# Batch 3's u turned on TensorE, v loaded from SyncE's queue, and the last output tile in two halves

## The chip, the cores and the metric

The kernel runs on one core of one Trainium2 chip. The metric is the device time of one execution in microseconds. Three timed runs of the kernel before took 314.05, 314.24 and 315.2 us; the median is 314.24 us. Engines are named as the profile names them: PE (TensorE), DVE (VectorE), ACT (ScalarE), POOL (GpSimd) and SP (SyncE). SP only issues transfers.

## The reference

Eight batches of 576 tokens go through attention with 8 heads of 64 (a band of 32 tokens on each side, and 8 global tokens), and the result x through a mixer: first across the tokens, then across the 512 channels.

```python
mask = np.abs(pos[:, None] - pos[None, :]) <= window          # window = 32
mask = mask | is_global[:, None] | is_global[None, :]
attn = softmax(where(mask, scale * q @ k.T, -1e9))
x = (attn @ v)                                                # [8, 576, 512]
h = np.maximum(xt @ w_tok1, 0.0) @ w_tok2                     # xt: x with tokens last
u = x + h.transpose(0, 2, 1)
out = u + np.maximum(u @ w_ch1, 0.0) @ w_ch2                  # 512 -> 1536 -> 512
```

## The kernel before

Each batch has 576 tokens, handled as four tiles of 128 and a rest of 64; the rests of two batches share a tile of 128 rows. A batch passes these steps.

- `load_qk`, `load_rest`, `load_v` bring q, k and v as float32 (lq, lk, lr, lv: lr holds the rests of q and k, lv has five chunks). ACT casts them to float16 (qk, rn, vsh); DVE copies v to half-shifted rows (`shift_v`, tile vod).
- q and k are turned so that the head dimension lies on the partitions. For batches 0 to 2 PE does it (`turn_pe`); from batch 3 on nine DMA transposes from SP do (`turn_dma`, tiles rawr and raw), and DVE copies each result into qT and kT (L646 to L654).
- `scores` (L673), an exponential on ACT (L683, tile e), a mask on DVE (L689), the sums for the global tokens (L720), `values` (L740, L753), and a division on DVE give x (L781).
- `token1` (L803, tile a) and `token2` (L821) are the mix across tokens; DVE adds x and gives u (L834), and ul for the rest (L837).
- `turn_u` turns u to uT with the channels on the partitions: for b < 3 by four PE transposes a tile (L848) and an eviction by ACT or DVE (L850), otherwise by one DMA transpose a tile from SP (L853). The shared rest is always turned by a DMA transpose (L843, tile uTl).
- `chan1` (L866; L878 for the rest) with a relu (L858, L860; tiles b, b1l), then `chan2` (L895): 12 matmuls a tile of tokens; DVE adds u and writes osb (L903), and POOL, or SP for the last batch and for the rests, stores it (L906, L909).

All this is recorded by `op` as a list of operations, each with the engines it may run on and a cost in microseconds, a priority, and what it reads and writes. `run` then plays a model of the core over the list: at each step it takes the operation with the lowest priority number among those that could start soonest on an engine, and writes out that engine's instruction. So the order on every engine is fixed when the program is built, and a changed cost or engine can move other operations too. At run time each engine works strictly in its written order and waits at semaphores. A transfer issued by SP or ACT also waits for an earlier one of SP or ACT, since completions are counted on eight semaphores that are used in turn.

Eight PSUM banks are shared by everything PE writes; `run` gives a bank to a new result when its former result has been read. There is one lv for all batches, so a chunk of the next batch is loaded once ACT has cast the one before. From batch 3 on q and k are loaded by SP and v by ACT (L942 to L946). With `manual_schedule` nothing else reorders.

The last operations are batch 7's: `chan2` of its four tiles, each stored by SP, and the shared rest of batches 6 and 7, which SP stores in two pieces of 64 rows.

Of the kernel before, what the change touches and what calls it, by code (L numbers as in the profile page):

```python
# [8 lines left out]
F32 = mybir.dt.float32  # L9
# [6 lines left out]
P = 128  # L16
# [11 lines left out]
def kernel(  # L28
# [12 lines left out]
    nc = tc.nc  # L41
    B, H, S, D = q.shape
# [5 lines left out]
    NJ = DCH // P  # L48
    assert S == 576 and D == 64 and DM == 512 and DTOK == 256 and DCH == 1536
    LAST = S - P * (NT - 1)  # L50
# [68 lines left out]
    def run(free, look, hop, warm_until):  # L119
# [41 lines left out]
        def drain(t):  # L161
            if t > clock[0]:
                flow(rings, clock[0], t)
                clock[0] = t
# [28 lines left out]
        while ready:  # L193
            cand = {}
            for i in ready:
                o = ops[i]
                t0, sl = 0.0, None
                if o["new"]:
                    sl = slot(o["new"][0], len(o["new"][1]), max([free["P"]] + list(at[i].values())))
                    if sl is None:  # L200
                        continue
                    t0 = max(t0, max(x[0] for x in sl))
                best = None
                for k, (e, c) in enumerate(o["opts"]):
                    st = max([free[e], t0] + [f + (hop if x != e else 0.0) for x, f in at[i].items()])
                    if o["dma"]:
                        ln, z = lanes["G" if e == "G" else "S"], filled["A" if e == "K" else e]
                        if len(ln) >= 8:
                            st = max(st, max(ln[-8], ln[-7], ln[-6]) + 2.5 if e == "A" else ln[-8])
                        room, x = RING - o["dma"][3], len(z)  # L210
                        while x and room >= z[x - 1][1]:
                            room -= z[x - 1][1]
                            x -= 1
                        if x:
                            st = max(st, z[x - 1][0])
                    if e == "P" and o["mode"] != mode:
                        c = c + 0.095
                    key = (st + c + 0.25 * k, e, st, c)
                    if best is None or key < best:
                        best = key  # L220
                cand.setdefault(best[1], []).append((best[2], o["pri"], i, best[3], sl))
            assert cand, ("stuck", banks, [(ops[i]["opts"], ops[i]["pri"], ops[i]["new"] and ops[i]["new"][1]) for i in ready])
            pick = None
            for e, cs in cand.items():
                lim = min(x[0] for x in cs) + look[e]
                x = min((x for x in cs if x[0] <= lim), key=lambda x: (x[1], x[0], x[2]))
                if pick is None or x[0] < pick[1][0]:
                    pick = (e, x)
            e, (st, _, i, c, sl) = pick
            o = ops[i]  # L230
            if e == "P":
                gap, spare = st - free["P"], [k for k in range(8) if (banks[k][1] is None or not open_uses[banks[k][1]]) and banks[k][0] <= free["P"]]
                if st < warm_until and gap > 0.52 and spare:
                    warm(min(spare, key=lambda k: (banks[k][0], k)), int((gap - 0.3) / (0.22 if st < 12.0 else 0.12)))
                mode = o["mode"]
            if o["new"]:
                kind, keys, shape, dt = o["new"]
                for key, (_, k) in zip(keys, sl):
                    home[key] = [k, k + 1] if kind == "S" else [k]
                    for z in home[key]:  # L240
                        banks[z] = (0.0, key)
                    ps_tile[key] = view(k, shape, dt)
            o["fn"](e)
            free[e] = st + c
            f = st + c + LAT[e]
            if o["dma"]:
                work, size, lag, packets = o["dma"]
                q = "A" if e == "K" else e
                drain(min(f, min(free[x] for x in "GSA")))
                f = land(q, f, work, size, i)  # L250
                filled[q].append((f, packets))
                f += lag
                lanes["G" if e == "G" else "S"].append(f)
                f += o["late"] + (LATE if st > 36.0 else 0.3)
            fin[i] = f
            log.append((st, f, e, i, max(o["deps"], key=lambda x: fin[x]) if o["deps"] else None))
            ready.discard(i)
            for key in o["ps"]:
                open_uses[key] -= 1
                for z in home[key]:  # L260
                    banks[z] = (max(banks[z][0], f + hop), key)
            for u in users[i]:
                left[u] -= 1
                if i in ops[u]["behind"]:
                    at[u][e] = max(at[u].get(e, 0.0), st + c)
                else:
                    x = "D" if o["dma"] else e
                    at[u][x] = max(at[u].get(x, 0.0), f)
                if not left[u]:
                    ready.add(u)  # L270
# [614 lines left out]
    nout = [0]  # L885

    def chan2(b, tau, pri):
        i, key = b % 2, ("o", b, tau)
        last = tau == NT - 1
        js = [range(0, 4), range(4, 8), range(8, 12)] if b == 0 else [range(0, 6), range(6, 12)]  # L890
        for part, jr in enumerate(js):
            def f(e, jr=jr):
                for j in jr:
                    w = b1l[:, j, :] if last else b1[:, j, P * tau : P * tau + P]
                    nc.tensor.matmul(ps_tile[key], lhsT=w, rhs=wc2[:, j, :], start=(j == 0), stop=(j == NJ - 1))  # L895
            r = [("wc2", t) for t in sorted({j // 4 for j in jr})]
            r += [("b1l", t) for t in range(3)] if last else [("b1", j) for j in range(NJ)]
            op([("P", 0.2165 * len(jr))], pri - 0.5 * part if b else pri + 5 * part, f, r=r, ps=[key], new=("M", [key], [P, 512], F32) if part == 0 else None)
        o = nout[0] % 3
        nout[0] += 1  # L900
        osb = osbs[o]
        def g(e):
            nc.vector.tensor_add(out=osb, in0=uls[b // 2 % 2] if last else u16s[i][:, tau], in1=ps_tile[key])  # L903
        op([("V", 0.62)], pri - 8, g, r=[("ul", b // 2 % 2, 0), ("ul", b // 2 % 2, 1)] if last else [("u", i, tau)], ps=[key], w=[("osb", o)])
        if not last:
            op([("G", 0.56) if b < B - 1 else ("S", 0.45)], pri + 5, lambda e: ENG[e].dma_start(out=out[b, P * tau : P * tau + P, :], in_=osb), r=[("osb", o)], dma=STORE)  # L906
        else:
            for z in range(2):
                op([("S", 0.45)], pri + 5, lambda e, z=z: nc.sync.dma_start(  # L909
                    out=out[b - 1 + z, S - LAST : S, :], in_=osb[64 * z : 64 * z + 64]), r=[("osb", o)], dma=(0.39, 2048, 0.8, 64))  # L910
# [11 lines left out]
    def loads(b, n0=0):  # L922
        pl = 100.0 * b - 145 if b != 1 else -174.0
        if b == 0:
            load_rest(0, -196, [("S", 0.65)])
            for hs in (slice(0, 2), slice(2, 4), slice(4, 8)):
                for ti in range(2):
                    load_qk(0, ti, hs, -195 + hs.start, [("S", 0.6)])
            load_v(0, -180, [("S", 0.6)])
            gate(-178, [("lv", NT - 4)], [lv[:, NT - 4, 0, 0:1]])  # L930
            return
        if b < PEB:
            if b == 1:
                pl = -173.9
            load_rest(b, pl, [("G", 0.73)], [n0] if b == 1 else ())
            for h in range(0, H, 4):
                for ti in range(2):
                    load_qk(b, ti, slice(h, h + 4), pl + 1 + h / 2 if b > 1 else pl + 0.1 + h / 100, [("G", 0.88)], [n0] if b == 1 else ())
            if b > 1:
                load_v(b, pl + 6, [("G", 0.87)])  # L940
        else:
            load_rest(b, pl, [("S", 0.65)])  # L942
            for h in range(0, H, 4):
                for ti in range(2):
                    load_qk(b, ti, slice(h, h + 4), pl + 1 + h / 2, [("S", 0.5)])
            load_v(b, pl + 6, [("A", 0.6)])  # L946

    def casts(b):
        pc = 100.0 * b - 140
# [6 lines left out]
    for b in range(B):  # L956
        base = 100.0 * b
        ca = base - 85
# [53 lines left out]
        for tau in range(NT):  # L1012
            token2(b, tau, ca + tau)
            if tau < NT - 1 or b % 2:
                turn_u(b, tau, ca + tau + 2, b < 3)
        if b and b % 2 == 0:
            chan2(b - 1, NT - 1, base + 24)
        for j in range(NJ):
# [40 lines left out]
```

## Time and profile before

| | |
|---|---|
| median of three timed runs | 314.24 us |
| profiled execution | 314.6 us |
| its span, first to last instruction | 312.9 us |
| PE / DVE / ACT / POOL busy in it | 292.0 / 186.8 / 180.5 / 60.5 us |
| mean granted PE clock | 0.987 of full speed |
| transfers: SP and ACT queues (q1, q10), POOL queue (q0) | 26.49 and 5.90 MB, 18.45 MB |

"L895 PE MATMUL bank<-wc,b" is a group of instructions by line of the kernel, engine, operation, what it writes and what it reads. In the views that list a timeline, a row has the start and the duration in us, the engine, the line and, in brackets, how long the engine stood idle before it and what released it; SPq and ACTq are transfers issued by SP and ACT, whose duration is that of the issue. A row of the windows view has the stretch, its length, the busy time and number of instructions of PE, PEld (weight loads), DVE, ACT and POOL, then the granted PE clock, the share of the transfer engines and GB/s. Batch b's channel step runs beside the scores of batch b + 1 and the transposes of batch b + 2: around 100 us PE is at token2 of batch 2, and around 136 us at that of batch 3.

### The profile page before, as it was taken

What the parts mean: (1) busy time and instruction counts of PE and PEld (TensorE: products, weight loads), DVE (VectorE), ACT (ScalarE), POOL (GpSimd) and SP (SyncE); (2) the same over time, 40 slices, a digit from 0 to 9 for tenths busy, and PEclk for the clock granted to TensorE, in tenths of its full rate; (3) what the DMA queues carried; (4) which work ended last, traced back from release to release, by engine and by line L of the source; (5) the groups of instructions that cost most, each with busy time, mean ns of one, the idle gap of its engine ahead of it and who ended that gap; (6) DMA issues with size and microseconds to landing.
All of it is one profiled execution on the core that took longest, in us unless ns stands there. A gap on an engine that the chain in (4) does not pass through costs nothing.

```text
span 312.9 us, 7276 instructions
## 1 busy us (share of the span) xinstructions
PE 292.0 (93%) x2943; PEld 154.4 (49%) x2943; DVE 186.8 (60%) x410; ACT 180.5 (58%) x325; POOL 60.5 (19%) x109
## 2 busy tenths in 40 slices
PE   6979889997999979988999998999999999999994
PEld 4755545454474434533456444544555445444641
DVE  7789667569686674876675846964543357230021
ACT  4864895377987758841989376733742083305500
POOL 8589635632001100002000110002000200020000
PEclk9989999999999979999999999999999999999998
DMA  6989999999999999999979999924003211051013
GB/s 183 255 129 287 208 222 222 287 243 234 214 212 220 194 267 318 118 190 221 325 114 176 203 313 189 159 50 136 36 0 63 89 53 37 12 140 69 2 67 102
DMA packets 94660, 51.31 MB, mean 164 GB/s; under 512 B 73698, under 2 KB 89954, under 8 KB 94626
## 3 DMA queue, kind: packets, MB, share of 16 engines
q1 hardware_dynamic: 62480, 26.49, 40.3%
q0 software_dynamic: 8704, 18.45, 24.0%
q10 hardware_dynamic: 23442, 5.90, 11.1%
q8 instruction: 23, 0.38, 0.5%
q14 instruction: 11, 0.09, 0.1%
HBM read 36.11 MB, written 9.44 MB: 146 GB/s over the span
## 4 chain that ended last, share of the span: by engine, by line
PE 58%; DMA 26%; ACT 5%; DVE 5%; issue 2%; SPq 2%; POOL 1%; POOLq 0%; ACTq 0%; DVEq 0%
PE bank L895 22%; PE bank L866 21%; DMA lv<-in_v_dram 8%; DMA raw<-qk 6%; DMA lq<-in_q_dram 5%; PE bank L821 4%; DMA g_q<-in_q_dram,idx_i 3%; PE bank L673 3%; PE bank L803 2%; DMA lk<-in_k_dram 2%; PE bank L878 2%; ACT qk L534 2%; ACT vsh L546 2%; DVE osb L903 2%; PE bank L753 1%
## 5 line engine op out<-in xcount | busy, mean ns | idle before, releaser
L866 PE MATMUL bank<-uT,wc 128*128 128x512 f16 x384 | 94.0, 384 | 6.4 <-DVE osb L903 2.3
L895 PE MATMUL bank<-wc,b 128*128 128x512 f16 x384 | 88.3, 379 | 2.9 <-DVE osb L903 2.2
L858 ACT ACTIVATE b<-bank 128x512 f16<-128x512 f32 x88 | 52.5, 617 | 38.3 <-PE bank L866 38.3
L683 ACT ACTIVATE e<-bank 128x648 f16<-128x648 f32 x64 | 42.7, 737 | 30.0 <-PE bank L673 29.8
L895 PEld LDWEIGHTS <-b 128*128 128x128 f16 x384 | 36.7, 98 | 45.9 <-issue 4.2
L866 PEld LDWEIGHTS <-wc 128*128 128x128 f16 x384 | 35.2, 98 | 48.5 <-issue 8.7
L906 POOL DMA_DIRECT2D out_dram<-osb x28 | 16.1, 574 | 203.1 <-DVE osb L903 203.0
L903 DVE TENSOR_TENSOR osb<-u,bank 128x512 f32<-128x512 f16 x32 | 21.9, 686 | 45.3 <-PE bank L895 41.5
L546 ACT CAST vsh<-lv 128x512 f16<-128x512 f32 (+3 forms) x44 | 26.5, 620 | 9.7 <-DMA uT<-u 5.3
L689 DVE TENSOR_TENSOR e<-e,masku 128x1296 f16<-128x1296 f16 x28 | 23.3, 831 | 13.7 <-ACT e L683 13.2
L834 DVE TENSOR_TENSOR u<-x,bank 128x512 f16<-128x512 f16 x30 | 18.7, 681 | 15.0 <-PE bank L821 14.8
L781 DVE TENSOR_TENSOR x<-bank,rr 128x512 f16<-128x512 f32 x32 | 22.1, 691 | 1.1
L821 PE MATMUL bank<-a,w 128*128 128x512 f16 x80 | 20.1, 379 | 0.5 <-DVE a L809 0.3
L534 ACT CAST qk<-lq 128x512 f16<-128x512 f32 x26 | 16.2, 626 | 4.5 <-DMA lq<-in_q_dram 2.0
L803 PE MATMUL bank<-x,w 128*128 128x512 f16 x64 | 18.7, 379 | 0.0
L673 PEld LDWEIGHTS <-kT 64*128 64x128 f16 x576 | 11.2, 97 | 14.4 <-issue 13.6
L534 ACT CAST qk<-lk 128x512 f16<-128x512 f32 x27 | 16.9, 631 | 1.8 <-DMA lk<-in_k_dram 1.8
L654 DVE COPY qT<-raw 128x512 f16<-128x512 f16 x20 | 12.0, 602 | 7.2 <-DMA raw<-qk 7.1
L753 PEld LDWEIGHTS <-e 128*64 128x64 f16 x576 | 16.1, 116 | 0.1
L740 PE MATMUL bank<-rf,lf 128*64 128x264 f16 x144 | 15.6, 293 | 0.5 <-DVE rf L726 0.5
L753 PE MATMUL bank<-vsh,e 128*64 128x66 f16 x320 | 16.0, 199 | 0.0
L673 PE MATMUL bank<-qT,kT 64*128 64x72 f16 x576 | 15.4, 198 | 0.0
(164 smaller groups left out, 333.6 us busy)
## 6 DMA issues: line engine op xcount, KB each, us to landing
out_dram<-osb POOLq DMA_DIRECT2D x28, 256.0 KB, 4.3
lq<-in_q_dram SPq DMA_DIRECT2D x11, 512.0 KB, 6.4
lk<-in_k_dram SPq DMA_DIRECT2D x11, 512.0 KB, 7.9
lv<-in_v_dram ACTq DMA_DIRECT2D x15, 256.0 KB, 4.6
wc<-in_moe_w_ch_dram POOLq DMA_DIRECT2D x6, 512.0 KB, 12.8
lq<-in_q_dram POOLq DMA_DIRECT2D x4, 512.0 KB, 6.4
lk<-in_k_dram POOLq DMA_DIRECT2D x4, 512.0 KB, 11.0
lv<-in_v_dram ACTq DMA_DIRECT2D x10, 192.0 KB, 3.8
```

Of the source, the lines that this page charges most:

```text
L534: COPY[e](out=qk[:, ti, p].rearrange("q i (r d) -> q r i d", r=2), in_=(lq, lk)[ti][:, hs])
L546: COPY[e](out=vsh[i][a:z, c, :, 0:D], in_=lv[a:z, c])
L673: nc.tensor.matmul(ps_tile[keys[z]][:, u // 3, UW * (u % 3) : UW * (u % 3) + UW], lhsT=kT[r, 64 * u : 64 * u + P], rhs=qT[r, u // 2, UW * ...
L683: op([("A", 0.595)], pri + 1, lambda e, par=par: nc.scalar.activation(out=es[i][:, 2 * p + par].rearrange("p (n u) x -> p n u x", n=3), in ...
L689: op([("V", 0.85)], pri + 2, lambda e: nc.vector.tensor_mul(out=e2, in0=e2, in1=masku.unsqueeze(1).to_broadcast([P, 2, NB, UW])), r=["mask ...
L753: nc.tensor.matmul(o[:, VW * hh : VW * hh + VW], lhsT=es[i][:, h, 2 * tau + c, x : x + 64], rhs=vod[i][:, tau, h, :] if c else vsh[i][:, t ...
L803: nc.tensor.matmul(ps_tile[key][:, tt], lhsT=w, rhs=x16s[i][:, ch, :], start=(ch == 0), stop=(ch == NT - 1))
L821: nc.tensor.matmul(ps_tile[key], lhsT=w2[:, ch, P * tau - sh : P * tau - sh + P], rhs=a1[:, ch, :], start=(ch == 0), stop=(ch == 1 and not ...
L858: nc.scalar.activation(out=out, in_=in_, func=AF.Relu)
L866: nc.tensor.matmul(ps_tile[key], lhsT=wc1[:, cc, P * j : P * j + P], rhs=uT[:, cc, :], start=(cc == 0), stop=(cc == 3))
L895: nc.tensor.matmul(ps_tile[key], lhsT=w, rhs=wc2[:, j, :], start=(j == 0), stop=(j == NJ - 1))
L903: nc.vector.tensor_add(out=osb, in0=uls[b // 2 % 2] if last else u16s[i][:, tau], in1=ps_tile[key])
```

## The change

Four edits. `turn_u` is called with PE for b < 4 instead of b < 3, so batch 3's four full tiles of u are turned by PE. `load_v` of batches 3 to 7 goes to SP instead of ACT, with a cost of 1.0 in the model instead of 0.6; the cost of a `load_qk` on SP becomes 1.15 instead of 0.5. The last tile, the shared rest of batches 6 and 7, is made in two halves of 256 columns, each with 12 matmuls of 256 columns, its own PSUM bank and its own add; of each half SP stores the 64 rows of batch 6 and ACT those of batch 7. And in the model a transfer issued by ACT holds SP for a time that grows with its packets; after the change this touches only the stores of the last tile.

```diff
@@ run
             if o["dma"]:
                 work, size, lag, packets = o["dma"]
                 q = "A" if e == "K" else e
+                if e == "A":
+                    free["S"] = max(free["S"], st) + 0.9 * o["dma"][3] / 1024
                 drain(min(f, min(free[x] for x in "GSA")))
@@ chan2
         last = tau == NT - 1
+        if last and b == B - 1:
+            osb = osbs[nout[0] % 3]
+            for z in range(2):
+                cs, kz = slice(256 * z, 256 * z + 256), ("o", b, tau, z)
+                def f(e, cs=cs, kz=kz):
+                    for j in range(NJ):
+                        nc.tensor.matmul(ps_tile[kz], lhsT=b1l[:, j, :], rhs=wc2[:, j, cs], start=(j == 0), stop=(j == NJ - 1))
+                op([("P", 1.31)], pri + z, f, r=[("wc2", t) for t in range(3)] + [("b1l", t) for t in range(3)], ps=[kz], new=("M", [kz], [P, 256], F32))
+                op([("V", 0.4)], pri - 8, lambda e, cs=cs, kz=kz: nc.vector.tensor_add(out=osb[:, cs], in0=uls[b // 2 % 2][:, cs], in1=ps_tile[kz]),
+                   r=[("ul", b // 2 % 2, 0), ("ul", b // 2 % 2, 1)] + ([] if z else [("osb", nout[0] % 3)]), ps=[kz], w=[("osbz", z)])
+                for y in range(2):
+                    op([("SA"[y], 0.45)], pri + 5 + z, lambda e, y=y, cs=cs: ENG[e].dma_start(
+                        out=out[b - 1 + y, S - LAST : S, cs], in_=osb[64 * y : 64 * y + 64, cs]), r=[("osbz", z)], dma=(0.25, 1024, 0.8, 64))
+            return
@@ loads
-                    load_qk(b, ti, slice(h, h + 4), pl + 1 + h / 2, [("S", 0.5)])
-            load_v(b, pl + 6, [("A", 0.6)])
+                    load_qk(b, ti, slice(h, h + 4), pl + 1 + h / 2, [("S", 1.15)])
+            load_v(b, pl + 6, [("S", 1.0)])
@@ the loop over batches
-                turn_u(b, tau, ca + tau + 2, b < 3)
+                turn_u(b, tau, ca + tau + 2, b < 4)
```

The order of other instructions moves with it. In the lists below a line number of the new kernel is 2 higher than the old one up to `chan2`, and 16 higher behind it.

SP, around the transposes of batch 4 (rawr from the rests rn, raw from qk; the lq and lk ahead load batch 4). Before:

```order
L643 DMA_TRANSPOSE raw<-qk 128x4x128 x4
L504 DMA lq<-in_q_dram 128x4x256
L504 DMA lk<-in_k_dram 128x4x256
L639 DMA_TRANSPOSE rawr<-rn 128x4x128
L643 DMA_TRANSPOSE raw<-qk 128x4x128 x8
```

After:

```order
L645 DMA_TRANSPOSE raw<-qk 128x4x128 x5
L506 DMA lk<-in_k_dram 128x4x256
L506 DMA lq<-in_q_dram 128x4x256
L506 DMA lk<-in_k_dram 128x4x256
L525 DMA lv<-in_v_dram 96x8x64
L525 DMA lv<-in_v_dram 128x8x64 x3
L525 DMA lv<-in_v_dram 96x8x64
L641 DMA_TRANSPOSE rawr<-rn 128x4x128
L645 DMA_TRANSPOSE raw<-qk 128x4x128 x8
```

Five loads of batch 4's v now stand ahead of its nine transposes, and one load of k has gone behind the last transposes of batch 3.

DVE, at the outputs of batch 1 (osb from u_1, batch 1's u) beside the copies of batch 4's turned q and k into qT_72 and kT_74. Before:

```order
L903 TENSOR_TENSOR osb_104<-u_1_95,bank 128x512
L654 COPY qT_72<-raw 128x4x128
L903 TENSOR_TENSOR osb_102<-u_1_95,bank 128x512
L651 COPY kT_74<-raw 128x512
L654 COPY qT_72<-raw 128x4x128
L651 COPY kT_74<-raw 128x512
L654 COPY qT_72<-raw 128x4x128
L903 TENSOR_TENSOR osb_103<-u_1_95,bank 128x512
L689 TENSOR_TENSOR e_81<-e_81,masku 128x1296
```

After:

```order
L919 TENSOR_TENSOR osb_104<-u_1_95,bank 128x512
L648 COPY qT_72<-rawr 128x4x64
L650 COPY kT_74<-rawr 128x4x64
L556 COPY vod_78<-vsh_76 64x2112
L919 TENSOR_TENSOR osb_102<-u_1_95,bank 128x512
L653 COPY kT_74<-raw 128x512
L919 TENSOR_TENSOR osb_103<-u_1_95,bank 128x512
L656 COPY qT_72<-raw 128x4x128 x2
L691 TENSOR_TENSOR e_81<-e_81,masku 128x1296
```

The last output of batch 1 stood behind five copies from raw and now stands behind one, the second of the eight transposes; a copy of batch 4's v (vod_78) has come ahead of it.

DVE, between x and the first output of the next stage, at batch 3 (u_1 and ul_97 are batch 3's, osb from u_0 is batch 2's, kT_75 and qT_73 batch 5's). Before:

```order
L651 COPY kT_75<-raw 128x512
L654 COPY qT_73<-raw 128x4x128
L860 TENSOR_SCALAR b_100<-bank 128x512
L625 COPY gT<-bank 128x128
L628 COPY kgz<-bank 64x16x8 x2
L633 COPY qT_72<-gT 128x20x8
L651 COPY kT_75<-raw 128x512
L633 COPY qT_73<-gT 128x20x8
L654 COPY qT_73<-raw 128x4x128
L834 TENSOR_TENSOR u_1_95<-x_1_92,bank 128x512 x4
L837 TENSOR_TENSOR ul_97<-x_1_92,bank 64x512
L903 TENSOR_TENSOR osb_102<-u_0_94,bank 128x512
```

After:

```order
L862 TENSOR_SCALAR b_100<-bank 128x512
L627 COPY gT<-bank 128x128
L630 COPY kgz<-bank 64x16x8 x2
L635 COPY qT_72<-gT 128x20x8
L648 COPY qT_73<-rawr 128x4x64
L650 COPY kT_75<-rawr 128x4x64
L656 COPY qT_73<-raw 128x4x128
L653 COPY kT_75<-raw 128x512
L836 TENSOR_TENSOR u_1_95<-x_1_92,bank 128x512 x4
L839 TENSOR_TENSOR ul_97<-x_1_92,bank 64x512
L653 COPY kT_75<-raw 128x512
L656 COPY qT_73<-raw 128x4x128
```

The first row of the old list has four more copies ahead of it (rawr's pair, a vod copy and a raw copy); in the new one the copies of two raw tiles come ahead of u instead of five, and two more between ul and the output.

## The prediction

> **What bounds the kernel now.** I read the page first: its shares and its chain.
>
> ```profile
> span 312.9 us, 7276 instructions
> PE 292.0 (93%) x2943; PEld 154.4 (49%) x2943; DVE 186.8 (60%) x410; ACT 180.5 (58%) x325; POOL 60.5 (19%) x109
> ```
>
> PE is the bound, with 20.9 us idle in the span. The second view, PE's waits from 95 to 200 us, says where idle time is left that this change can reach (before 95 us the queues hardly differ, and after 200 us the list of PE's waits is empty):
>
> ```profile
> PE bank L895 <- DVE osb L903: 2.2, 2, 1.8
> PE bank L866 <- DVE osb L903: 2.1, 1, 2.1
> PE bank L720 <- DVE eg L692: 0.8, 1, 0.8
> PE bank L895 <- ACT b1l L858: 0.4, 1, 0.4
> PE bank L895 <- DVE u L834: 0.2, 1, 0.2
> PE bank L821 <- DVE b L860: 0.2, 1, 0.2
> ```
>
> That is 5.9 us, and it is DVE that is late, not a load as such. The third view, PE's granted clock in short windows, adds a hidden cost:
>
> ```profile
> 113.00:114.00 1.00, 0.73 (x2) 0.24 (x2) 0.96 (x3) 0.00 (x0) 0.49 (x1) 0.66 0.90 199
> 114.00:115.00 1.00, 1.00 (x3) 0.15 (x1) 1.00 (x3) 0.00 (x0) 0.05 (x1) 0.50 0.99 187
> 115.00:116.00 1.00, 1.00 (x20) 0.69 (x20) 0.97 (x4) 0.79 (x2) 0.00 (x0) 0.50 0.73 150
> 116.00:117.00 1.00, 1.00 (x4) 0.39 (x3) 1.00 (x3) 1.00 (x2) 0.00 (x0) 0.63 1.01 369
> ...
> 142.00:144.00 2.00, 2.00 (x10) 0.91 (x10) 1.97 (x4) 0.40 (x1) 0.56 (x1) 1.00 1.31 240
> ```
>
> After the 2.1 us stop the clock (third number from the end) is 0.66, 0.50, 0.50, 0.63, so 0.34 + 0.50 + 0.50 + 0.37 = 1.71 us of work is lost. After the 1.8 us stop at 141.9 it stays 1.00. So the first stop costs 2.08 + 1.71 = 3.79 us, and all of them together 7.6 us. The Trainium skill ("TensorE: Matmul & The Clock Gate", "What's actually happening") has the clock halve after an idle window of about 3.4 us; by that a 2.1 us stop costs no clock, and the sum below would lose 1.71 us of gain. The trace shows 0.50 after 2.1 us, so the trace decides.
>
> Why PE stops there is read from DVE's and SP's timelines:
>
> ```profile
> 107.52 0.61 DVE L651 COPY kT<-raw 128x512 f16<-128x512 f16 x1 [0.26 <-DMA raw<-qk]
> 109.65 0.62 DVE L654 COPY qT<-raw 128x512 f16<-128x512 f16 x1 [1.52 <-DMA raw<-qk]
> 112.03 0.59 DVE L654 COPY qT<-raw 128x512 f16<-128x512 f16 x1 [1.25 <-DMA raw<-qk]
> 112.54 0.68 DVE L903 TENSOR_TENSOR osb<-u,bank 128x512 f32<-128x512 f16 x1
> ```
>
> ```profile
> 97.22 0.57 SPq L504 DMA_DIRECT2D lq<-in_q_dram  x1
> 97.84 0.50 SPq L504 DMA_DIRECT2D lk<-in_k_dram  x1
> 98.45 1.19 SPq L639 DMA_TRANSPOSE rawr<-rn  x1
> 99.75 12.26 SPq L643 DMA_TRANSPOSE raw<-qk  x8
> ```
>
> DVE works strictly in order. The add at 112.54 frees the PSUM bank that PE's chan1 of batch 2 needs; it stands behind copies of batch 4's transposes, which SP issues one per 12.26 / 8 = 1.53 us. The second lands at 107.52, the fifth at 112.03, and only the fifth lets the add go.
>
> **The change part by part.** The sum is made against the profiled execution, 312.9 us of span and 314.6 us in all, 0.4 us over the median of 314.24; differences are carried to the median.
>
> *1. The stop at 111 us.* In the new DVE order this add waits for the second raw tile of batch 4 instead of the fifth; rawr and one vod copy stand ahead of it too. But SP now issues five loads of batch 4's v ahead of rawr; each waits until ACT has cast batch 3's v out of the same buffer, and behind them on SP stand all nine transposes, for which DVE waits. What one costs on SP is not in this stretch of the trace. The nearest rows:
>
> ```profile
> L523 ACTq DMA_DIRECT2D lv<-in_v_dram x25: 337/391/1265, 69.2 to 199.4; - x25
> 5.57 9.06 SPq L523 DMA_DIRECT2D lv<-in_v_dram  x5
> 105.00:113.00 8.00, 6.06 (x65) 2.60 (x64) 4.78 (x10) 5.15 (x10) 1.23 (x2) 1.00 1.27 222
> ```
>
> Below, 0.39 us each, as on ACT; above, 9.06 / 5 = 1.81, as on SP at the start. I take 0.57, the load on SP at 97.22, same queue and moment. The second tile then lands at 107.52 + 5 x 0.57 = 110.4, the bank is free at 110.4 + 0.60 + 0.68 = 111.7 instead of 113.2, 1.5 us earlier, and with the stop at 0.6 us the clock stays up. Gain 1.5 + 1.71 = **3.2 us**. Bounds: 3.8 at 0.39 (the stop gone), and at 1.81 the tile lands at 116.6, 4.6 us after 112.03: a loss of 4.6. What the 25 moved issues free on ACT is not on the path: ACT mostly waits for PE there.
>
> *2. The stop at 142 us.* DVE again:
>
> ```profile
> 134.75 0.61 DVE L654 COPY qT<-raw 128x512 f16<-128x512 f16 x1 [2.50 <-DMA raw<-qk]
> 137.96 2.48 DVE L834 TENSOR_TENSOR u<-x,bank 128x512 f16<-128x512 f16 x4
> 140.47 0.69 DVE L837 TENSOR_TENSOR ul<-x,bank 64x512 f16<-64x512 f16 x1
> 141.19 0.69 DVE L903 TENSOR_TENSOR osb<-u,bank 128x512 f32<-128x512 f16 x1
> ```
>
> Between batch 3's x and that add the new order has one vod copy (0.70) and one raw copy (0.60) less, and only the first two tiles of batch 5 ahead of u. But PE comes earlier by part 1, and SP's stream of batch 5 again has v loads ahead. Bounds: the whole 1.78 + 0.19 + 0.16 = 2.1 us won, or none. I take **1.0 won**, the middle, since DVE's own work shrinks by 1.3.
>
> *3. u of batch 3 on PE.* Added 16 transposes of 128x128; removed four DMA transposes on SP:
>
> ```profile
> 101.63 0.32 PE bank L848 x4
> 292.54 2.69 PE bank L878 x48
> 138.68 5.15 SPq L853 DMA_TRANSPOSE uT<-u  x4
> L850 ACT COPY uT<-bank 128x512 f16<-128x512 f16 x11 | 6.3, 589 | 2.4 <-PE bank L848 2.3
> ```
>
> The same instruction took 0.32 / 4 = 0.08 us, a stream of that size 2.69 / 48 = 0.056. So 0.9 to 1.3 us; I take **1.3 lost**. Four evictions of 0.59 go to ACT, 2.4 us, covered by PE's 36 matmuls of chan2 that stand there anyway (7.8 us); without that cover they would cost the 2.4. The 5.15 us that SP wins only makes batch 6's loads earlier, which nothing waits for at 138 us: nothing.
>
> *4. v on SP in the later batches.* The one stop there, at 192 us, hangs on a transpose:
>
> ```profile
> 181.25 2.10 SPq L639 DMA_TRANSPOSE rawr<-rn  x1
> 190.33 0.23 DVE L646 COPY qT<-rawr 128x256 f16<-128x256 f16 x1 [2.03 <-DMA rawr<-rn]
> ```
>
> Now lk and five v loads stand between uT and this rawr, and PE comes 3.2 + 1.0 - 1.3 = 2.9 us earlier. Between the 0.8 us stop vanishing and 5 x 0.57 = 2.9 us being added, I take **0.7 lost**, because the uT ahead of them, waiting for u, also moves earlier with PE.
>
> *5. The tail.*
>
> ```profile
> 295.23 12.96 PE bank L895 x60
> 308.22 0.69 DVE osb L903
> ...
> 308.93 1.12 SPq L909 DMA_DIRECT2D out_dram<-osb  x2
> DMA to landing us min/median/max: 2.3/2.3/2.4
> ...
> L789 DVE TENSOR_TENSOR x<-bank,rr 64x256 f16<-64x256 f32 x16 | 6.8, 422 | 0.4
> lv<-in_v_dram ACTq DMA_DIRECT2D x15, 256.0 KB, 4.6
> ```
>
> 24 matmuls of half the width keep the array as long as 12 (12 x 0.216 = 2.6). The last add covers 256 columns: 0.42 instead of 0.69. The two last stores start together at 308.65 instead of the second at 308.93 + 0.56 = 309.5. **0.86 won**, if a store from ACT lands as one from SP. If it took the 4.6 us of ACT's loads, it would land at 313.2 instead of 311.8: 1.4 lost.
>
> Sum: -3.2 - 1.0 + 1.3 + 0.7 - 0.9 = -3.1 us, so 314.24 - 3.1 = **311.1 us**.
>
> **The rivals.** *A, slower: v's loads hold up the transposes behind them.* The place is part 1; it decides from (112.03 - 107.52) / 5 = 0.90 us per load. For it: SP's own v loads took 1.81, and five of them are 1152 KB, 5.3 us at the 222 GB/s of that window, 1.06 each, if what follows waits for their data. Against: its q and k loads took 0.5 to 0.6 in that stretch. At 1.06 the tile lands at 112.8, the bank comes 0.8 us later than before, the clock falls as before, and part 2 wins nothing: +0.8 + 1.3 + 0.7 - 0.9 = +1.9, **316.1 us**; at 1.81, 320. The Trainium skill ("DMA: Bandwidth & Descriptors", "Queues, rings and completion order") bears on it: an engine takes turns between queue rows, so v on a row of its own shares, while on SP's row what comes later queues behind it; this trace shows no v on SP beside transposes.
>
> *B, no change: the gain is given back.* PE's order is fixed and the transposes of batches 5 to 7 come at SP's pace; if they don't move, PE waits at 192 us for what it won, and only the tail is left: 314.24 - 0.9 = **313.4 us**. For it: the chain before 192 runs over a raw transpose. Against: SP is rid of 5.15 us at 138 us, and ACT of all issues, so the pace can move.
>
> *C, more: all the stops go.* -7.6 + 1.3 - 0.9 = -7.2, **307.0 us**. For it: DVE's copies are spread; against: every copy ahead of an add is still a possible wait.
>
> **How the numbers follow.** Forecast 0.56, A 0.14, B 0.17, C 0.13. The range leaves out A and the lowest of C, 307.2 to 314.8. About 0.5% (1.6 us) is what a measurement here can tell from no change. Faster: C 0.13, nearly all of the forecast 0.54, a little of B 0.03, together 0.70; same 0.17; slower 0.13.
>
> **What would show it.** Right: no clock window under 0.9 between 105 and 120 us, PE's wait for osb there under 1 us, SP's v loads near 0.6 us each, the last store issued by 308.7 less what was won. Wrong: v loads on SP over 0.9 us, a raw copy with a wait of 2 us ahead of an osb add, or a stop of over 2 us at L720 or L866 later. A stop in front of token2 of batch 2 (near 98 us), where the order now has the last tile of batch 3 ahead of the first add, would be one that I have left at nothing (its 0.4 us stop stays).

## The result, and the profile after

The changed kernel takes 322.69 us (median, 322.39 to 324.27) against 314.24 us: 1.027 times the kernel before, with a 95% interval of 1.0235 to 1.0304. Forecast were 311.1 us. The change costs 8.4 us where 3.1 were to be won. Times in this document are medians of all runs of a kernel, and ratios compare its fast runs alone, since some runs lie over 1.5% above the fastest of their kernel.

The first two rows of the page, to be read beside those of before:

```profile
span 322.5 us, 7368 instructions
PE 294.0 (91%) x2971; PEld 156.0 (48%) x2971; DVE 187.6 (58%) x410; ACT 182.9 (57%) x330; POOL 60.5 (19%) x109
```

PE is busy 2.0 us more and idle 28.5 us in place of 20.9. PE's waits over the whole span (us in total, times, the longest one); the rows left out at the "..." are waits of 1.9 us each on qT and rf:

```profile
PE bank L911 <- DVE u L836: 3.3, 1, 3.3
PE bank L722 <- DVE eg L694: 3.2, 3, 2.0
PE bank L868 <- DVE osb L919: 2.9, 1, 2.9
...
PE bank L911 <- DVE osb L919: 1.5, 1, 1.5
PE bank L823 <- DVE osb L919: 1.4, 1, 1.4
```

It is still DVE that is late. Where the time goes, batch by batch, shows the start of the pair of divisions that completes x of a batch (the `x` rows of DVE at L789 before, L791 after), read from both timelines:

| | x of batch 2 | 3 | 4 | 5 | 6 | 7 | end of the span |
|---|---|---|---|---|---|---|---|
| before, us | 91.6 | 128.5 | 163.5 | 199.0 | 229.3 | 264.9 | 312.9 |
| after, us | 93.5 | 130.4 | 166.2 | 209.6 | 239.7 | 275.3 | 322.5 |
| late by | 1.9 | 1.9 | 2.8 | 10.6 | 10.4 | 10.4 | 9.6 |

Of the 9.6 us, 7.8 arise between x of batch 4 and x of batch 5. The place on which the forecast's largest term rested, between x of batches 2 and 3, neither wins nor loses.

The trace points to SP. All v loads in one row, and SP's timeline where batch 4's v stands ahead of its transposes:

```profile
L525 SPq DMA_DIRECT2D lv<-in_v_dram x30: 449/1237/4781, 5.6 to 193.1; - x30
```

```profile
97.16 0.57 SPq L506 DMA_DIRECT2D lk<-in_k_dram  x1
97.78 0.50 SPq L506 DMA_DIRECT2D lq<-in_q_dram  x1
98.33 0.51 SPq L506 DMA_DIRECT2D lk<-in_k_dram  x1
98.93 7.74 SPq L525 DMA_DIRECT2D lv<-in_v_dram  x5
106.78 1.32 SPq L641 DMA_TRANSPOSE rawr<-rn  x1
108.66 10.96 SPq L645 DMA_TRANSPOSE raw<-qk  x8
```

The q and k loads take 0.5 to 0.57 us, as the forecast took for v as well. The five v loads behind them take 7.74 / 5 = 1.55 us each, and rawr goes out at 106.78 in place of 98.45. DVE then stands still for it, with the adds that PE wants behind:

```profile
113.15 0.23 DVE L648 COPY qT<-rawr 128x256 f16<-128x256 f16 x1 [6.46 <-DMA rawr<-rn]
...
114.28 0.69 DVE L919 TENSOR_TENSOR osb<-u,bank 128x512 f32<-128x512 f16 x1
114.89 0.60 DVE L653 COPY kT<-raw 128x512 f16<-128x512 f16 x1
115.40 0.68 DVE L919 TENSOR_TENSOR osb<-u,bank 128x512 f32<-128x512 f16 x1
```

The first of these adds frees PE, only at 115.0 (the stop of 2.88 us, L868). Batch 3 shows the same earlier: its v loads stand on SP from 69.46 us on, its rawr goes out at 80.99 in place of 77.90, and rf, which PE needs, stands behind the copies:

```profile
86.53 0.23 DVE L648 COPY qT<-rawr 128x256 f16<-128x256 f16 x1 [1.21 <-DMA rawr<-rn]
...
87.96 0.70 DVE L728 TENSOR_TENSOR rf<-bank,blk 128x528 f16<-128x528 f32 x1
```

Before, these two rows stood at 83.88 and 86.43; PE now stops for 1.42 us ahead of L742. Batch 6 shows it on a larger scale. SP, with the row of the kernel before for the same eight transposes behind it:

```profile
150.05 1.34 SPq L506 DMA_DIRECT2D lk<-in_k_dram  x1
151.49 9.03 SPq L525 DMA_DIRECT2D lv<-in_v_dram  x3
...
164.15 2.93 SPq L641 DMA_TRANSPOSE rawr<-rn  x1
167.18 11.57 SPq L645 DMA_TRANSPOSE raw<-qk  x8
```

```profile
159.57 11.37 SPq L643 DMA_TRANSPOSE raw<-qk  x8
```

Three v loads took 9.03 us, and batch 6's transposes start 7.6 us later than before, while x of batch 4 is only 2.8 us later. What DVE and PE make of it:

```profile
178.70 0.59 DVE L656 COPY qT<-raw 128x512 f16<-128x512 f16 x1 [0.60 <-DMA raw<-qk]
179.32 2.48 DVE L836 TENSOR_TENSOR u<-x,bank 128x512 f16<-128x512 f16 x4
181.72 0.67 DVE L839 TENSOR_TENSOR ul<-x,bank 64x512 f16<-64x512 f16 x1
182.32 0.67 DVE L919 TENSOR_TENSOR osb<-u,bank 128x512 f32<-128x512 f16 x1
```

```profile
180.06 1.46 PE L911 MATMUL bank<-wc,b 128*128 128x512 f16 x6 [3.33 <-DVE u L836]
183.04 5.34 PE L911 MATMUL bank<-wc,b 128*128 128x512 f16 x24 [1.52 <-DVE osb L919]
```

u of batch 4 stands behind seven copies from raw, the last of which waits for a transpose until 178.70; PE stops for 3.33 and 1.52 us. In the kernel before, five such copies stood ahead of this u, and u waited for PE, not for a copy; the written order has changed here too. At 187.35 the five loads of batch 7's v follow, and PE stops again, for 2.02 us from 199.1 on, behind a copy from rawr at 199.91 for which DVE had waited 4.00 us.

### The profile page after: what moved, and what is told of

It reads as the page before. It is cut to its first block, busy times and chain, and to the rows that moved or that the text cites. A ratio compares the mean times of both kernels' runs of the same rounds, so it can differ in the third digit from the quotient of the medians.

```text
span 322.5 us, 7368 instructions
## 1 busy us (share of the span) xinstructions
PE 294.0 (91%) x2971; PEld 156.0 (48%) x2971; DVE 187.6 (58%) x410; ACT 182.9 (57%) x330; POOL 60.5 (19%) x109
## 4 chain that ended last, share of the span: by engine, by line
PE 48%; DMA 17%; ACT 15%; DVE 12%; issue 4%; SPq 2%; POOL 0%; ACTq 0%
PE bank L911 17%; PE bank L868 16%; ACT e L685 5%; DMA lk<-in_k_dram 4%; DMA raw<-qk 4%; DMA rawr<-rn 4%; ACT b L860 3%; PE bank L823 3%; DMA g_k<-in_k_dram,idx_i 2%; PE bank L805 2%; PE bank L675 2%; ACT vsh L548 2%; PE bank L755 2%; PE bank L880 2%; PE bank L742 2%
## 5 line engine op out<-in xcount | busy, mean ns | idle before, releaser
L868 PE MATMUL bank<-uT,wc 128*128 128x512 f16 x384 | 93.8, 383 | 5.4 <-DVE osb L919 2.9
L868 PEld LDWEIGHTS <-wc 128*128 128x128 f16 x384 | 35.2, 98 | 47.3 <-issue 8.8
L742 PE MATMUL bank<-rf,lf 128*64 128x264 f16 x144 | 15.4, 290 | 2.4 <-DVE rf L728 1.9
L653 DVE COPY kT<-raw 128x512 f16<-128x512 f16 x20 | 12.0, 599 | 5.4 <-DMA raw<-qk 5.2
```

Source lines behind the costliest of these rows:

```text
L868: nc.tensor.matmul(ps_tile[key], lhsT=wc1[:, cc, P * j : P * j + P], rhs=uT[:, cc, :], start=(cc == 0), stop=(cc == 3))
```

## The experiments

Three theories were set against each other. Theory 1, later called Q: v on SP's queue makes the transposes late. Theory 2: u of batch 3 on PE costs the time. Theory 3: the new written order is bad by itself. Ratios are to the kernel before, timed beside it on the same chip, with 95% intervals.

| kernel | us | ratio | interval |
|---|---|---|---|
| changed | 322.69 | 1.0269 | 1.0235 to 1.0304 |
| v on SP alone | 326.35 | 1.0474 | 1.0392 to 1.0556 |
| the same, v ahead of q and k | 315.76 | 1.0073 | 1.0025 to 1.012 |
| changed, v ahead of q and k | 313.84 | 0.9952 | 0.9918 to 0.9986 |
| changed, model's queue 2600 packets | 319.25 | 1.0168 | 1.0104 to 1.0231 |
| changed, half of v | 309.72 | 0.9813 | 0.9766 to 0.986 |
| before, half of v | 310.38 | 0.9885 | 0.982 to 0.995 |
| changed, raw told 4 us later | 324.44 | 1.0266 | 1.0216 to 1.0315 |
| changed, u of batch 3 by DMA | 324.43 | 1.0348 | 1.028 to 1.0416 |
| v ahead, u of batch 3 by DMA | 314.91 | 1.0013 | 0.9979 to 1.0048 |
| u on PE and halved tail, v on ACT | 317.62 | 1.0164 | 1.0082 to 1.0246 |
| halved tail alone | 313.47 | 0.9977 | 0.9917 to 1.0036 |
| halved tail, raw told 2 us later | 313.39 | 0.9957 | 0.992 to 0.9995 |
| v ahead, raw told 2 us later | 312.81 | 0.9978 | 0.9941 to 1.0014 |
| changed order, v issued by ACT | 339.08 | 1.0869 | 1.0758 to 1.098 |

**v on SP alone** (the kernel before with one edit):

```diff
-                    load_qk(b, ti, slice(h, h + 4), pl + 1 + h / 2, [("S", 0.5)])
-            load_v(b, pl + 6, [("A", 0.6)])
+                    load_qk(b, ti, slice(h, h + 4), pl + 1 + h / 2, [("S", 1.15)])
+            load_v(b, pl + 6, [("S", 1.0)])
```

> The kernel before with the third part of the change alone: v of batches 3 to 7 on SP's queue, with the model costs that go with it (1.0 for v, 1.15 for q and k). Theory 1 (a load of v holds SP for 1.2 us and more, since the queue is full, so the transposes behind it come late and DVE and PE wait): the whole loss and the tail's gain on top, 322 to 325 us, with stops of 2 us and more of PE behind DVE copies of raw. Theory 2 (the loss comes from u of batch 3 on PE, its evictions on ACT and the PE time): 314 us, no stop of 3 us near 178 us.

It takes 326.35 us, more than the whole change and more than either theory expected. So this edit alone makes the loss, and more. The parts don't simply add up: beside it the other edits give some of it back, and without it they cost 1.6% (u on PE and halved tail, below). Its v loads are as dear as in the changed kernel:

```profile
L523 SPq DMA_DIRECT2D lv<-in_v_dram x30: 339/1450/3502, 5.9 to 198.6; - x30
```

**The changed order, v issued by ACT** (only the engine that issues batch 3 to 7's v is put back):

```diff
-                ENG[e].dma_start(
+                (nc.scalar if b >= 3 else ENG[e]).dma_start(
                     out=lv[r0:r1, c], ...
```

> The changed kernel with the same written order on every engine, but each load of v of batches 3 to 7 is issued by ACT at its place in that order instead of by SP. Theory 1 (the price of v on SP's queue): the transposes come as early as before, 312 to 315 us. Theory 3 (the new order, made with other costs, is bad by itself, whichever queue carries v): 319 us or more.

All theories missed: 339.08 us. ACT's timeline and PE's show why it says little about the order:

```profile
116.63 0.34 ACTq L525 DMA_DIRECT2D lv<-in_v_dram  x1
117.01 0.62 ACT L536 CAST qk<-lq 128x512 f16<-128x512 f32 x1 [6.97 <-DMA raw<-qk]
```

```profile
118.65 0.58 PE L850 MATMUL bank<-ident,u 128*128 128x128 f16 x4 [6.60 <-ACT uT L852]
```

ACT stands for 6.97 us ahead of a v load, which the profile puts down to a completion of SP's transposes (the two share the semaphores that count completions), and the evictions of uT, for which PE waits, stand behind it: 6.60 us. In this run the order written for SP holds up ACT's computing. Theory 3 stays untested by it.

**u on PE and the halved tail, without v**, and **the tail alone** (the changed kernel with these lines put back; the second also with the last pair):

```diff
-                if e == "A":
-                    free["S"] = max(free["S"], st) + 0.9 * o["dma"][3] / 1024
-                    load_qk(b, ti, slice(h, h + 4), pl + 1 + h / 2, [("S", 1.15)])
-            load_v(b, pl + 6, [("S", 1.0)])
+                    load_qk(b, ti, slice(h, h + 4), pl + 1 + h / 2, [("S", 0.5)])
+            load_v(b, pl + 6, [("A", 0.6)])
...
-                turn_u(b, tau, ca + tau + 2, b < 4)
+                turn_u(b, tau, ca + tau + 2, b < 3)
```

> The changed kernel without the move of v: u of batch 3 on PE and the halved last tile, v on ACT and the model costs as before. Theory 1: 16 transposes on PE cost up to 1.3 us, the tail wins 0.9, so 313.5 to 315 us; less, if the stop at 142 us goes. Theory 2 (u on PE causes the loss): 320 us or more.

> The kernel before with the last tile in two halves stored by SP and ACT, nothing else. All theories: 0.9 us faster (313.3 us), the last store issued about 0.85 us earlier; if ACT's store landed like its loads of v, 1.4 us slower.

317.62 and 313.47 us; the first lies between what the two theories expected. The tail wins 0.2%, which the interval doesn't tell from nothing. u on PE costs some 4 us here by the medians, and 1.9%, nearer 6 us, by the ratios: three times or more the 1.3 that were taken. A wait that the kernel before doesn't have is u itself: PE's transposes of batch 3's u stand in PE's order and wait for DVE.

```profile
138.53 0.40 PE L848 MATMUL bank<-ident,u 128*128 128x128 f16 x4 [2.53 <-DVE u L834]
```

**Half of v** (in the changed kernel, and in the kernel before; heads 4 to 7 of v of batches 3 to 7 are left out, so these two kernels don't compute the reference; bytes and pieces of v are halved, and the instructions stay):

```diff
+                hs = slice(0, 4 if b >= 3 else H)
-                    out=lv[r0:r1, c], in_=v[b, :, j0 : j0 + (r1 - r0), :].rearrange("h p d -> p h d")
+                    out=lv[r0:r1, c, hs], in_=v[b, hs, j0 : j0 + (r1 - r0), :].rearrange("h p d -> p h d")
```

> The changed kernel, but v of batches 3 to 7 is loaded for heads 0 to 3 only (the other half of lv keeps batch 2's values), so each of the 25 loads on SP has half the pieces and bytes; number and order of all instructions stay. Theory Q (SP's queue takes an issue at once while little is outstanding in it, and makes SP wait when much is; what costs is the amount of v in front of the transposes in one queue): the five issues at 98.9 us took 7.74 us and fall by more than half, to 2.5 to 3.5 us; batch 4's transposes start about 4 us earlier; the time falls from 322.7 to between 313 and 317. Theory S (a v load is dear to issue on SP in itself, per issue): the issues stay at 1.2 us and more, 7 us for the five, and the time stays at 320 to 323. If the price goes by pieces alone, the five take 3.9 us.

> The kernel before (v on ACT), but v of batches 3 to 7 is loaded for heads 0 to 3 only; the other half of lv keeps batch 2's values. It tells whether the 309.7 us of the half-v run on SP came from less traffic in general or from less in SP's queue. Theory Q: on ACT's row the bytes hardly matter to SP's transposes, 312 to 315. Theory B (the transfer engines as a whole are the limit, busy over 90% up to 200 us): this kernel gains as well, 306 to 310.

```profile
94.74 5.44 SPq L526 DMA_DIRECT2D lv<-in_v_dram  x5
```

The five issues at this place fall from 7.74 to 5.44 us only, not to 2.5 to 3.5, but the kernel falls by 13 us, to 309.72, below all theories. PE's waits from 80 to 215 us (this kernel's lines are one higher than the changed kernel's) show that the stops of 3.33, 2.88 and 2.02 us are gone:

```profile
PE bank L824 <- ACT a L815: 2.1, 1, 2.1
PE bank L912 <- DVE osb L920: 0.8, 1, 0.8
PE bank L743 <- ACT b L861: 0.6, 1, 0.6
PE bank L824 <- DVE osb L920: 0.2, 1, 0.2
```

The kernel before gains too, 1.15% or 3.6 us (310.38 us), so less traffic helps on ACT's row as well: theory B holds in part. The pair is what counts: with half of v the change as a whole costs nothing (0.9813 against 0.9885, intervals that overlap), with the whole of v 2.7%. The amount of v on SP is what costs, not the number of issues. It is also the test of theory 3: the written order on every engine is that of the changed kernel, so the order by itself, with less v in SP's queue, loses nothing.

**v ahead of q and k**:

```diff
-            load_v(b, pl + 6, [("S", 1.0)])
+            load_v(b, pl - 0.9, [("S", 1.0)])
```

> The changed kernel with v's priority ahead of the q and k loads of its batch: five v loads stand in front of lk, lq, lk and batch 4's transposes; for later batches the plan puts v directly behind the last batch's transposes. Theory Q: of the five v loads the first two take about 0.5 us, and the three q and k loads behind them, 0.57, 0.50 and 0.51 us in the changed kernel, take over 1 us each; rawr starts at 107 us, give or take 1, as it does now. Later batches' transposes have had more time, so the time falls a little, 316 to 321. Theory S: every v load takes 1.2 us or more, the q and k loads stay at 0.5 to 0.6 us, and rawr starts at 107 us too; 320 to 323.

313.84 us: the whole loss is gone with one priority, better than either theory had it. Which issues are long goes with what is already in the queue:

```profile
97.39 3.98 SPq L525 DMA_DIRECT2D lv<-in_v_dram  x5
101.42 0.85 SPq L506 DMA_DIRECT2D lk<-in_k_dram  x1
102.31 0.54 SPq L506 DMA_DIRECT2D lq<-in_q_dram  x1
102.90 0.61 SPq L506 DMA_DIRECT2D lk<-in_k_dram  x1
103.63 2.46 SPq L641 DMA_TRANSPOSE rawr<-rn  x1
```

The same eight loads take 97.16 to 106.67 us in the changed kernel, 9.5 us, and 97.39 to 103.51, 6.1 us, in this one. The trace's packets show how full the queue was. A q or k load here makes 512 packets of 1 KB, a v load 768 or 1,024 of 256 bytes, a transpose 512 of 256 bytes; with these numbers SP's issues add up to the 80,384 data packets of queue q1. Packets issued less packets finished, at the start and the end of each issue:

```
changed kernel                          v ahead of q and k
start   us    load  at start  at end    start   us    load  at start  at end
 97.2  0.57   lk       502      574      97.4  0.53   lv       489      839
 97.8  0.50   lq       537     1024      98.0  0.49   lv       780     1792
 98.3  0.51   lk      1024     1523      98.6  0.53   lv      1791     2621
 98.9  0.45   lv      1510     2178      99.2  0.95   lv      2541     2596
 99.5  1.38   lv      2148     2712     100.3  1.10   lv      2488     2224
101.0  2.61   lv      2682     2715     101.4  0.85   lk      2172     1946
103.7  1.22   lv      2629     2531     102.3  0.54   lq      1910     1949
105.0  1.67   lv      2425     2292     102.9  0.61   lk      1912     1931
```

Counted so from 40 us on, the fullest that SP's queue became was 2,582 to 2,755 packets in the nine kernels with the whole of v on SP, and 2,085 at most in those with v on ACT. Over the nine kernels, the 40 v loads that began with fewer than 1,000 packets outstanding took 0.47 to 0.64 us each; of the 87 that began with 2,000 or more, 75 took over 1 us. In between both kinds stand, 33 of 98 over 1 us, so the runs show no sharp threshold; at 61.63 us of the changed kernel a q load that began with 2,046 packets took 4.58 us. While such an issue lasts, SP waits with all that follows.

q and k are few packets with many bytes, v many packets with few. That v's loads have to wait for the 1.5 MB of q and k where these stand in front would explain why v in front is quicker; no run shows it by itself. Theory Q was right on the first loads (0.53, 0.49) and wrong on what follows: q and k stay at 0.85 us and less, and rawr goes out at 103.63, not at 107. Theory S falls, for a v load of 1,024 packets takes 0.49 us at 98.0 here and 4.78 at 155.74 in the changed kernel. The gain comes at batch 6, whose rawr copies go from 169.94 to 165.17, so that u of batch 4 starts at 173.42 in place of 179.32, with seven copies from raw ahead of it as in the changed kernel; this u stops PE no longer:

```profile
172.79 0.60 DVE L656 COPY qT<-raw 128x512 f16<-128x512 f16 x1 [0.31 <-DMA raw<-qk]
173.42 2.48 DVE L836 TENSOR_TENSOR u<-x,bank 128x512 f16<-128x512 f16 x4
```

Part of that lead is another order of the loads too: one v load of batch 6 goes out 20 us sooner, and batch 7's rests later. And the written order of DVE and ACT moves with the priority. How much is the queue's fullness and how much the rest isn't separated.

**v on SP alone, ahead of q and k**, the first experiment with only v's priority changed (the edit is shown against that kernel):

```diff
-            load_v(b, pl + 6, [("S", 1.0)])
+            load_v(b, pl - 0.9, [("S", 1.0)])
```

> The kernel before with one edit, v of batches 3 to 7 on SP, placed ahead of q and k of its batch (model costs 1.0 and 1.15 us). The same edit with v behind q and k took 326.3 us (1.047). If the place in SP's queue is what costs, nearly all of that goes: 313 to 317. If the u and tail edits are what made the other v-first kernel good (313.8), this one stays slow: 320 to 327.

315.76 us in place of 326.35, and the median v load 0.90 in place of 1.45 us. By the ratios, v's place, with the order that moves with it, is worth 4.0 of the 4.7% that the edit costs; 0.7% is left.

```profile
L523 SPq DMA_DIRECT2D lv<-in_v_dram x30: 338/897/3378, 6.2 to 184.7; - x30
```

**The model told of the queue** (`RING`, the number of packets that the model lets a queue hold):

```diff
-    RING, LATE = 4096, 2.0
+    RING, LATE = 2600, 2.0
```

> The changed kernel with one number of the planner's model changed: a queue holds 2600 packets at most, in place of 4096 (counted from the trace of the changed kernel, SP's queue never held over 2,715 outstanding packets, and issues become long when it holds over 2,000). SP's written order then puts parts of v between the transposes. Theory Q (the price of v on SP is its place in a queue that is full): the issues of lv fall below 1 us in the median (1.24 in the changed kernel), and the time falls to 312 to 318. Theory S (the loads are dear wherever they stand): 320 to 324.

319.25 us, just above the range of theory Q. SP's order now mixes v loads and transposes, the median v load falls to 0.93 us, and 3.4 us of the 8.4 come back. The number that the model took for the queue is part of why its order was bad, not all.

**The model told that q's and k's transposes land later** (by 4 us in the changed kernel, by 2 us in the kernel with the halved tail and in the one with v ahead; the argument is added to both kinds of transposes):

```diff
-                    r=[("qk", ti, p)], w=[("raw", ti, p)], dma=TURN)
+                    r=[("qk", ti, p)], w=[("raw", ti, p)], dma=TURN, late=4.0)
```

> The changed kernel, but the model is told that the DMA transposes of q and k land 4 us later. SP's order hardly changes; on DVE the adds of osb and u move ahead of copies from raw. Theory D (the late transposes cost PE time because DVE's written order has their copies in front of the adds that PE waits for): PE's stops at 115 us (2.9 us) and 180 us (3.3 us) go below 1 us each and the time falls to 314 to 319. Against it (the turned q and k are themselves needed that soon): those stops are replaced by stops of PE's scores on qT or kT, and the time stays at 321 to 325.

> The kernel before with the last tile in two halves, v on ACT, u as before, and the model told that the DMA transposes of q and k land 2 us later. Theory D: the stops at 111 and 142 us, which hang on the same copies, shrink in this kernel too: 309.5 to 312.5. Against it: the copies become late for the scores, or other adds wait; 313 to 316.

> v ahead of q and k, u of batch 3 on PE, halved tail, and the planner told that DMA transposes of q and k land 2 us later. PE's stops in the v-first kernel between 80 and 215 us are 1.7 (rf), 1.4 (u), 1.3 and 0.9 us (osb); if half of them go, 310 to 312.5; if other waits take their place, as with 4 us in the kernel with v behind q and k, 313 to 316.

324.44, 313.39 and 312.81 us. Theory D falls in the form in which it stood: the changed kernel is no faster. Its trace, of an execution of 327.0 us, shows no stop at 180 us any more, but at 112 to 116 us the adds now stand behind copies of v, and PE stops for 1.78 and 0.43 us there; further stops of 2 us and more hang on ACT. So it isn't shown what DVE's order alone is worth. The two small cases are within 0.5% of the kernels that they vary.

**u of batch 3 by DMA again**, in the changed kernel and with v ahead:

```diff
-                turn_u(b, tau, ca + tau + 2, b < 4)
+                turn_u(b, tau, ca + tau + 2, b < 3)
```

> The changed kernel without one of its edits: batch 3's u is turned by DMA transposes again (b < 3). Theory 2 (PE's 16 transposes and ACT's evictions cost 1.3 us, and free SP of 5 us): it moves by +1 to -1.5 us, 321 to 324. Theory Q: SP gets four more transposes at 138 us, where batch 6's loads stand behind them, and batch 4 and 5's stops grow by up to 5 us: 323 to 328.

> v ahead of q and k on SP (313.8 us measured with u of batch 3 on PE), but u of batch 3 turned by DMA transposes as in the kernel before. The pair without v on SP told that u on PE costs about 4 us (317.6 against 313.5). If that price holds here, 309 to 312; if it was that plan's own accident, 313 to 316.

324.43 and 314.91 us. Here u on PE comes out better by 0.8% in the changed kernel and by 0.6% with v ahead, both with intervals that overlap. In the pair with v on ACT it cost some 4 us. That the same 16 transposes are a gain where SP's queue is full, and a loss where it isn't, would fit; no run shows it by itself.

Of the kernels with the whole of v, the changed one with v ahead of q and k has the lowest ratio, 0.9952 (0.9918 to 0.9986). It beats the changed kernel clearly and the kernel before only by half a per cent; the halved tail with raw told 2 us later, at 0.9957 with v on ACT, can't be told from it.

## Why the prediction was wrong

By x of the batches, against the terms of the forecast:

| term | forecast, us | measured, us |
|---|---|---|
| up to x of batch 2 (batch 3's v on SP) | left at nothing | +1.9 |
| 1, the stop at 111, with the stop near 98 | -3.2 | 0 |
| 2 and 3, the stop at 142 and u on PE | -1.0 + 1.3 | +0.9 |
| 4, later batches' v | +0.7 | +7.8 |
| batches 5 to 7 | nothing | -0.2 |
| 5, the tail | -0.9 | -0.8 |
| sum | -3.1 | +9.6 |

*The step that failed is the duration of 0.57 us for a v load on SP, the term from which parts 1 and 4 are made.* It was taken from a q load in the same queue, and the row at the start of the program, 1.81, was kept as a bound only. Measured are 1.55 at this place, 1.24 in the median, and 4.78 at most. The forecast's own point of decision, 0.90 us, was passed, and rival A's mechanism is what happened: SP's later transposes, DVE's copies behind them, DVE's adds behind the copies. The trace of the kernel before had a nearer row than 0.57: one load each of q and k, with 2,043 and 1,925 packets outstanding ahead of them.

```profile
61.93 4.25 SPq L504 DMA_DIRECT2D lq<-in_q_dram  x1
66.35 2.89 SPq L504 DMA_DIRECT2D lk<-in_k_dram  x1
```

*The premise that before 95 us the queues hardly differ* was wrong as well: batch 3's v stands on SP from 69.46 us on, and the stop ahead of L742 is most of the 1.9 us lost there.

*Part 1* moved no time where it was to win 3.2 us. The new order on DVE did what it says; but rawr, not the second raw tile, held it, until 113.15 (110.4 was forecast for the tile). The stop grew from 2.08 to 2.88 us, and only the clock, which stayed up, made it no dearer. The stop ahead of token2 of batch 2, named as left at nothing, came: 1.44 us.

*Parts 2 and 3* came near as a sum in this kernel, +0.9 against +0.3, but that is in part luck: the runs show that part 3 is no constant. It came out between a gain of 0.8%, with intervals that overlap, and a loss of some 4 us.

*Part 4* is the largest miss, and not only by the 0.57. It priced one stop, at 192 us, with the loads of one batch. The 7.8 us arise from two batches' loads: batch 6's (the stops of 3.33 and 1.52 us at 180 and 183) and batch 7's (2.02 us at 201, and 1.71 of clock behind it). That is 8.6, less the 0.8 of the stop that stood there before. That five loads at 1.55 us would also make 7.8 is chance. The 5.15 us of SP's time that u's leaving freed at 138 us were more than used up by batch 6's v, 9.03 us for three loads.

*Part 5* was right: the last matmul ends at 318.61 and the span at 322.5, 3.9 us later; before it was 308.2 and 312.9, 4.7 us. The two stores of SP and ACT go out together.

```profile
315.83 2.78 PE L898 MATMUL bank<-wc,b1l 128*128 128x256 f16 x24
```

```profile
317.79 1.78 SPq L903 DMA_DIRECT2D out_dram<-osb  x2
```

Rival A itself was too cheap, 316.1 to 320: it priced its mechanism at part 1's place alone, and the trace shows it at batch 3 and, dearest, at batches 6 and 7 as well. Rival C fell; rival B's fear, that the transposes come at SP's pace, was the right one, but the pace became slower, not the same.

## What to carry to other kernels

Before a load is moved to another queue, count what stands in that queue in packets and in bytes at that place: here the issue of a v load took about 0.5 us in a nearly empty queue and up to ten times that in a full one. In this kernel the loads of many small packets were better ahead of the large ones. That transfers for which an engine waits (here the transposes) should go ahead of both is a guess that no run tests by itself. A moved load is priced at every stage in which it recurs, not only at the stop that it was meant to shorten.

## What the runs showed of the hardware that was not expected

SP's queue became no fuller than 2,755 packets in any kernel, and the issue of a v load of 1,024 packets took between 0.49 and 4.78 us, the long ones where 2,000 and more were outstanding in most cases. ACT's own row shows long issues too, where the changed order puts several v loads on it in a row: 3.31 us at 168.91 and 3.52 us at 173.07 in the run with v issued by ACT, where they began with 1,792 and 2,513 packets outstanding on that row, against a median of 0.39 in the kernel before. The Trainium skill ("DMA: Bandwidth & Descriptors", "Issuing engines are not separate DMA queues") says that issuing from several engines only saves the time to initiate a transfer, usually small beside the transfer itself. The measurement goes further: taking v from ACT's row to SP's, behind q and k, cost 4.7% by itself.

PE's clock did not follow the length of a stop. Windows of 1 us over the stop of 2.88 us, and behind the stop of 2.02 us at 199.1 to 201.2 us (third number from the end: granted clock):

```profile
114.00:115.00 1.00, 0.00 (x0) 0.00 (x0) 0.97 (x3) 0.00 (x0) 0.00 (x0) 1.00 0.67 129
115.00:116.00 1.00, 0.97 (x4) 0.38 (x4) 1.00 (x3) 0.00 (x0) 0.54 (x1) 1.00 0.40 80
...
202.00:203.00 1.00, 1.00 (x4) 0.39 (x3) 1.00 (x3) 0.01 (x1) 0.00 (x0) 0.54 0.33 67
203.00:204.00 1.00, 1.00 (x3) 0.29 (x2) 0.47 (x1) 0.58 (x1) 0.00 (x0) 0.50 0.64 129
```

The longer stop left it at 1.00, as did the stop of 3.33 us ahead of 180.06; the shorter one brought it to 0.50 (0.54, 0.50, 0.50 and 0.75 in four windows, 1.71 us lost). So the 1.71 us that the forecast added to the stop at 111 us were one draw, not a price of every stop over 2 us. The Trainium skill ("TensorE: Matmul & The Clock Gate", "What's actually happening") has the clock judged in windows of about 3.4 us that run free of the kernel. That two longer stops left the clock alone would fit this; that a stop of 2 us, shorter than one window, halves it doesn't follow from it.
